# Three resident slices of each half of the second expert weights, and six b in half rows

## The chip, the cores and the metric

The kernel runs on one core of a Trainium2 chip. The metric is the time of one execution on the device in microseconds (us). These units matter here: TensorE does the matrix products (PE, its weight loads PEld), VectorE (DVE), ScalarE (ACT) and GpSimd (POOL) work on elements, SyncE (SP) issues transfers, and 16 DMA engines carry them between HBM and the on-chip memory.

## The reference

Three layers follow each other. An attention over 8 batches b (512 tokens and 32 states each) gives 544 rows of 512 per b. A feed-forward layer with two weights follows, and then a soft mixture of 8 experts. The last one is where the change lies:

```python
logits = x @ phi
d = softmax of logits over the 4608 tokens
slot_input = (d.T @ x).reshape(E, S_per_e, D)
for e in range(E):
    h = np.maximum(slot_input[e] @ w1[e], 0.0)
    slot_out[e] = h @ w2[e]
c = softmax of logits over the 32 slots
return (c @ slot_out).astype(np.float32)
```

w2 is 8 experts of 1024 x 512 in float32, 16.8 MB. Every row of the output, 4608 x 512, is a mix of the 32 rows of slot_out, so nothing can be stored before slot_out is there, at least for a half of the 512 columns.

## The kernel before

The main part, up to about 400 us, runs over the 8 batches (hstep, tstep, estep, smblock); the change doesn't touch it. What follows is a tail.

Weights of the experts come in slices of 1 MB, 128 partitions x 2048. There are 16 of w1 (half an expert's columns each) and 16 of w2: slice e of w2 is the first 256 output columns of expert e, slice 8 + e the last 256. They are loaded by SP into whatever place has come free: give puts places into a list, and prefetch takes the next place for the next slice of the list `slices`. So the order of the list is the order of the loads. The list is the four pieces of the feed-forward weight, the 16 slices of w1, and w2 in `order`:

```python
r0 = CFG["r0"]
kept = [list(range(8 - r0, 8)), list(range(10 + r0, 16))]
order = [i for i in range(16) if i not in kept[0] + kept[1]] + kept[0] + kept[1]
```

The last six of the list are resident: ends loads them early, into six places of the tile gp. With r0 = 0 these are slices 10 to 15.

After w1 (line 1053) two generators do the second product, slot_out(0) for the first 256 columns and slot_out(1) for the last (line 1088), eight steps of one slice each. A last step evicts the sum (tile SO), spreads it with a small product (SR, line 1095) and evicts that into `so`. slot_out takes the resident slices first. The generators combine then do the last product of a group of b: `combine(0, ...)` the first 256 columns of two b at a time, `combine(1, ...)` the last 256, `combine(None, ...)` all 512 columns of one b, for the b in `whole`, and of the rows of the states. They write four PSUM banks (tiles oV, oH, oX, oE), evict them by turns on DVE (line 1128) and ACT, and issue the store on SP (line 1132; the rows of the states on POOL, line 1136). A half-row store is 512 KB in runs of 1 KB, a whole-row store 1 MB in runs of 8 KB.

In which order the generators step is a string of CFG: 0 and 1 are the slot_outs, c is combine(0); afterwards slot_out(1), combine(0), combine(None) and combine(1) are run to their end in this order. The SP queue is worked off in the order of the program, so a store that waits holds up all stores behind it.

Of the kernel before, what the change touches and what calls it, by code (L numbers as in the profile page):

```python
# [13 lines left out]
PSUM = bass.MemoryType.PSUM  # L14


CFG = {'no': 1, 'nl': 0, 'n0': (1, 12), 'nw': 512, 'nj': 'CABD', 'cw': (2, 2, 2, 4, 5, 6, 6, 7, 8, 8, 9, 11, 12, 13, 14, 15), 'pr': (0, 4, 6), 'a0n': 5, 'w1p': (), 'r0': 0, 'sw': 1, 'whole': (4, 5, 6, 7), 'em': 8, 'lE': (0, 5, 8, 11), 'sV': (0, 4, 9, 12), 'sE': (7, 11, 15), 'sS': (1, 3, 5, 7), 'sN': 13, 'sM': (14, 14), 'gv7': 'EESESSSEESSSEEEE', 'cpos': (0, 0, 1, 2, 2, 3, 3, 7, 8, 10, 10, 10, 14, 14), 'at0': (4, 4, 7, 7, 9, 13, 14, 14, 14, 15), 'lP0': ((0, 1), (1, 0), (3, 0), (3, 1)), 'lP1': ((1, 0), (1, 1), (2, 0), (2, 1), (3, 0)), 'gv1': 'EEEEEEEEEESEEEES', 'f32': (0, 1, 2, 3), 'wsm': 14, 'xsP': 1, 'eng': ('PE',), 'wt8': (7, 8, 9, 10, 11, 12, 13, 14), 'wte': 'DA', 'wb': 12, 'gv6': (3, 5, 15), 'lP': ((0, 0), (0, 1), (1, 0), (2, 0), (3, 1)), 'attA': (3, 3, 9, 9, 9, 10, 10, 12), 'attB': (1, 11, 11, 12, 13), 'attN': (14, 15), 'dv': (3, 7, 8), 'fl': -0.484375, 'hp': 2000, 'att7': (3, 5, 6, 7, 8, 10), 'og': 1, 'n3': 1, 'n3m': 10, 'wS': ('DP', 'PP', 'AD', 'PD', 'AP', 'DP', 'AP', 'AD', 'AD', 'DP', 'AD', 'AP', 'AP', 'AD', 'PD', 'AD'), 'xsm': 12, 'k0': 0, 'rg': 6, 'spg': 0, 'att0': 6, 'att': 7, 'V0': (1, 2, 4), 'Vn': (1, 2, 10), 'Vx': 12, 'wn': 'H', 'wsev': 'adad', 'conv': (4, 8, 9, 11, 12, 13, 19, 21, 24, 26, 28, 32, 36, 40, 44, 48, 52, 56, 60), 'todo': [1, 1, 1, 2, 0, 0, 0, 3, 0, 0, 2, 2, 1, 1, 0, 0], 'E0': ((0, 7), (0, 14), (0, 15), (1, 1)), 'T0': ((0, 9), (0, 14), (1, 1), (1, 2)), 'sm0': 6, 'E': 1, 'sm': 1, 'tqB': (5, 9, 13), 'GP': 0, 'pe': (3,), 'psH': 3, 'gtpX': (0, 7), 'tq0': (13, 15), 'keep': (2, 3, 4, 5), 'x2': (1, 0), 'natm': 1, 'warm': 26, 'bounce7': (0, 3), 'split': 1, 'wt': 0, 'so': '1011110001000010c1cc1', 'smm': (0, 0, 1, 2, 8, 10, 12), 'tqv': (), 'tqvm': 0, 'first': 'x', 'apath': 2, 'f32c': 1, 'place': 1, 'attm': (3, 6, 7, 8, 9, 12), 'subPm': True, 'loDm': False, 'bounce': (0, 1, 2, 3), 'bq': ('s', 's'), 'xq': 's', 'nat': ((1, 11), (2, 2), (2, 3), (2, 11), (3, 2), (3, 4), (3, 9), (4, 2), (4, 3), (4, 9), (5, 2), (5, 3), (5, 9), (6, 2), (6, 4), (6, 9)), 'subP': (1,), 'mulD': (), 'loD': (), 'qlag': 0, 'gv0': 'SSEEEEEESEEEEEEE', 'gv': 'EEEEEEESEEEESEEE', 'gvS': 'BEBBBBBBBBBSBEBB'}


@with_exitstack  # L20
def kernel(
# [20 lines left out]
    def pool(name, bufs, **kw):  # L42
        return ctx.enter_context(tc.tile_pool(name=name, bufs=bufs, **kw))
# [6 lines left out]
    small = pool("small", 2)  # L50
    psH = pool("psH", CFG["psH"], space=PSUM)
    psE = pool("psE", 1, space=PSUM)
    psV = pool("psV", 1, space=PSUM)
    psX = pool("psX", 5 - CFG["psH"], space=PSUM)
    dram = pool("dram", 1, space=bass.MemoryType.DRAM)
# [58 lines left out]
    def group(calls, after=(), chain=False):  # L114

        first = mm(**calls[0])  # L116
        for i in after:
            tc.add_manual_dep(first.ins, i.ins.name, SYNC, reason="side by side")
        with tc.high_priority(CFG["hp"]):
            last = first  # L120
# [5 lines left out]
    def act(out, in_, func=ACTF.Copy, **kw):  # L126
        return nc.scalar.activation(out=out, in_=in_, func=func, **kw)  # L127
# [21 lines left out]
    def words(i, dst):  # L149

        w = stage[i].bitcast(U32).rearrange("p (f w) -> p f w", w=2)
        if i in CFG["dv"]:
            d = dst.bitcast(U32)
# [9 lines left out]
        r = rim.bitcast(U8).rearrange("p (f w) -> p f w", w=4)  # L163
        act(r[:, :, 0], b[:, :, 3], scale=2.0 ** -5, bias=CFG["fl"])
        if i in CFG["pr"]:
            nc.gpsimd.tensor_copy(out=r[:, :, 3], in_=b[:, :, 7])
# [1025 lines left out]
```

## Time and profile before

| | us |
|---|---|
| median of 3 runs | 481.89 (480.94 to 482.29) |
| profiled execution | 481.20 |
| its span | 479.4 |
| PE busy | 435.4 |
| DVE busy | 374.4 |
| ACT busy | 289.2 |
| POOL busy | 239.5 |

The span runs from the first to the last record; the profiled execution's own time is 1.8 us longer. Busy times of different engines overlap, and PE, the busiest, has nothing to do in the last 15 us, so shares over the whole span don't tell what sets the end. For that one reads stretches: the share of the DMA engines (a mean of 16, which can read a little above 1), and their rate in GB/s, microsecond by microsecond.

### The profile page before, as it was taken

To read this page: it belongs to the slowest core of one execution; us is meant where nothing else is said; L and a number is where in the kernel's file an instruction comes from. 1 tells how busy PE (TensorE), PEld (TensorE's weight loads), DVE (VectorE), ACT (ScalarE), POOL (GpSimd) and SP (SyncE) were. 2 spreads that over 40 slices of the span, in tenths; PEclk is the share of its full clock that TensorE was granted. 3 is DMA by queue.
4 is the path that set the end of the run, shared out by engine and by line. 5 is a ranking of instruction groups with operands and counts; after the bars stand their busy time and mean duration, and the time that the engine had idled before them with its cause. 6 is when DMAs were issued, how large, how long until landed. Compare 5 with 4: busy or idle time off the path is not lost.

```text
span 479.4 us, 10721 instructions
## 1 busy us (share of the span) xinstructions
PE 435.4 (91%) x4336; PEld 247.3 (52%) x4336; DVE 374.4 (78%) x667; ACT 289.2 (60%) x528; POOL 239.5 (50%) x217
## 2 busy tenths in 40 slices
PE   5689899999999999999999999999999997999850
PEld 2433345456565565655556555565557685435330
DVE  2999999896999998999799899878878655430260
ACT  1876996647775875886697587565654464220350
POOL 4243447865774973885497388464146231220030
PEclk9899999999999999999999999999999999999995
DMA  8999822011403613342351346025053598999698
GB/s 304 420 420 420 338 89 89 19 71 27 151 18 132 250 44 133 114 196 61 127 210 46 133 144 252 3 90 176 2 211 124 198 404 335 349 424 414 255 355 314
DMA packets 19809, 94.21 MB, mean 197 GB/s; under 512 B 1840, under 2 KB 6320, under 8 KB 11184
## 3 DMA queue, kind: packets, MB, share of 16 engines
q1 hardware_dynamic: 19504, 93.00, 51.0%
q8 instruction: 34, 0.56, 0.5%
q0 software_dynamic: 256, 0.52, 0.5%
q14 instruction: 15, 0.12, 0.1%
HBM read 80.41 MB, written 13.11 MB: 195 GB/s over the span
## 4 chain that ended last, share of the span: by engine, by line
PE 49%; DVE 28%; DMA 6%; ACT 5%; issue 5%; POOL 4%; ACTq 0%; SPq 0%; POOLq 0%; DVEq 0%
PE h L538 17%; DVE gp L612 6%; DVE g L592 5%; PE h L546 5%; PE E L116 3%; DMA w<-in_w_dram 3%; PE FV L122 3%; PE V L116 3%; PE h L1053 3%; POOL c L568 2%; PE h L529 2%; PE FX L122 2%; DVE mx L294 2%; DMA wb<-in_won_dram 2%; DVE z L335 1%
## 5 line engine op out<-in xcount | busy, mean ns | idle before, releaser
L538 PE MATMUL h<-a,v 128*128 128x512 f32 x672 | 175.5, 405 | 2.3 <-DVE g L592 2.0
L568 POOL TENSOR_TENSOR c<-c 128x512 f32<-128x512 f32 x106 | 114.6, 1084 | 97.1 <-ACT c L127 95.3
L538 PEld LDWEIGHTS h<-a,v 128*128 128x128 f32 x672 | 120.3, 188 | 77.9 <-issue 19.5
L127 ACT ACTIVATE c<-h,half 128x512 f32<-128x512 f32 x128 | 88.3, 691 | 71.0 <-PE h L538 54.6
L592 DVE SCALAR_TENSOR_TENSOR g<-h,c 128x512 f32<-128x512 f32 x112 | 74.7, 668 | 20.1 <-POOL c L568 17.0
L612 DVE STREAM_TRANSPOSE gp<-g 128x512 f32<-128x512 f32 x112 | 78.0, 699 | 1.1
L485 POOL TENSOR_TENSOR v<-Vs,v 128x512 fp32r<-128x512 f32 x30 | 41.7, 1389 | 9.5 <-ACT Vs L127 9.5
L127 ACT ACTIVATE v<-V 128x512 fp32r<-128x512 f32 (+1 forms) x64 | 38.1, 602 | 8.1 <-PE V L122 4.1
L116 PE MATMUL V<-win,st_t 64*32 64x512 f32 x64 | 34.0, 611 | 4.1 <-ACT att L127 3.7
L122 PE MATMUL V<-win,st_t 64*32 64x512 f32 x448 | 36.3, 612 | 0.0
L122 PE MATMUL FX<-gp,dR 32*32 32x512 f32 x512 | 35.6, 598 | 0.0
L122 PE MATMUL FV<-gp,dR 32*32 32x512 f32 x496 | 35.4, 597 | 0.0
L529 PE MATMUL h<-spare,v 128*128 128x512 f32 x64 | 32.5, 644 | 2.2 <-DVE gp L592 2.0
L122 PE MATMUL E<-g,wp 128*32 128x512 f32 x168 | 29.5, 602 | 0.0
L116 PE MATMUL E<-g,wp 128*32 128x512 f32 x56 | 29.1, 602 | 0.0
L337 POOL TENSOR_TENSOR att<-att,z 128x512 f32<-128x512 f32 x16 | 17.2, 1076 | 18.1 <-DVE z L336 18.1
L546 PE MATMUL h<-XSh,v 128*128 128x256 f32 x128 | 25.2, 289 | 0.1
L127 ACT ACTIVATE spare<-wb 128x512 uint8<-128x512 uint8 x32 | 24.0, 785 | 1.0 <-DMA wb<-in_won_dram 1.0
L1128 DVE COPY o<-oV 128x512 f32<-128x512 f32 x5 | 3.5, 691 | 26.5 <-PE oH L122 26.3
L529 PEld LDWEIGHTS h<-spare,v 128*128 128x128 f32 x64 | 11.9, 202 | 20.2 <-issue 13.5
L546 PEld LDWEIGHTS h<-XSh,v 128*128 128x128 f32 x128 | 20.2, 189 | 2.6 <-DVE g L592 0.8
L375 POOL TENSOR_TENSOR a<-att,a 128x512 fp32r<-128x512 f32 x14 | 19.6, 1418 | 1.1 <-ACT a L127 1.1
(245 smaller groups left out, 813.9 us busy)
## 6 DMA issues: line engine op xcount, KB each, us to landing
w<-in_w_dram SPq DMA_DIRECT2D x22, 1024.0 KB, 9.6
xn<-in_xn_dram SPq DMA_DIRECT2D x8, 1024.0 KB, 4.8
wb<-in_won_dram SPq DMA_DIRECT2D x8, 1024.0 KB, 5.0
xs<-in_xs_dram SPq DMA_DIRECT2D x7, 1024.0 KB, 4.8
gp<-in_w_dram SPq DMA_DIRECT2D x6, 1024.0 KB, 7.4
gp<-in_wout_dram SPq DMA_DIRECT2D x5, 1024.0 KB, 11.7
wb<-in_win_dram SPq DMA_DIRECT2D x4, 1024.0 KB, 12.8
wo<-wb SPq DMA_DIRECT2D x8, 512.0 KB, 3.7
```

The source lines that it names most:

```text
L116: first = mm(**calls[0])
L122: e = mm(**c)
L127: return nc.scalar.activation(out=out, in_=in_, func=func, **kw)
L337: (nc.vector if b in CFG["mulD"] else nc.gpsimd).tensor_tensor(out=t3, in0=t3, in1=z1.unsqueeze(2).to_broadcast([128, 16, 32]), op=ALU.mult)
L375: (nc.vector if b in CFG["loD"] or b > 1 and CFG["loDm"] else nc.gpsimd).tensor_tensor(out=lo[:, G, :], in0=raw[G], in1=hi[:, G, :], op=AL ...
L485: nc.gpsimd.tensor_tensor(out=lo[:, G, :], in0=Vs, in1=hi[:, G, :], op=ALU.subtract)
L529: mm(out=h, lhsT=Vt[0, c][0][:, G, 128 * mm_:128 * mm_ + 128], rhs=araw[0][G], start=(G == 0), stop=(G == 1))
L538: mm(out=h, lhsT=v[:, G, f], rhs=a[:, G, :], start=(k == 0), stop=(k == 5))
L546: mm(out=h, lhsT=w[:, j, :], rhs=x[:, j, :], start=(k == 0), stop=(k == 11))
L568: nc.gpsimd.tensor_tensor(out=c, in0=c, in1=c, op=ALU.mult)
L592: gI[b, m] = nc.vector.scalar_tensor_tensor(out=g, in0=h, scalar=1.0, in1=c, op0=ALU.max, op1=ALU.min)
L612: nc.vector.transpose(out=gd_of(b, m), in_=gT[b, m])
```

## The change

Three entries of CFG are changed; no other line is.

```diff
 CFG = {
...
-'r0': 0, 'sw': 1, 'whole': (4, 5, 6, 7),
+'r0': 3, 'sw': 1, 'whole': (6, 7),
...
-'so': '1011110001000010c1cc1',
+'so': '111000000000ccc111111',
...
```

With r0 = 3 the resident slices are 5, 6, 7 and 13, 14, 15, and the ten others are loaded in the order 0 to 4, 8 to 12. With whole = (6, 7) the b 0 to 5 are combined in pairs and stored in half rows, and 6 and 7 in whole ones. The string runs the three resident steps of slot_out(1), all of slot_out(0), the three pairs of combine(0), and the rest of slot_out(1).

On PE, at the end of slot_out(0): w_5_4620 is slice 5 of w2 (the last number is that of the buffer), SO the sum, SR its spreading, oV the first bank of the combine. Lines with - are before, with + after.

```order
-L1088 MATMUL SO<-w_5_4620,hTD 32x256 x8
-L1088 MATMUL SO<-w_6_4626,hTD 32x256 x8
-L1088 MATMUL SO<-w_7_4632,hTD 32x256 x8
-L1088 MATMUL SO<-w_8_4638,hTD 32x256 x4
+L1088 MATMUL SO<-w_8_4620,hTD 32x256 x8
 L1095 MATMUL SR<-tail,cst_t 128x256
-L1088 MATMUL SO<-w_8_4639,hTD 32x256 x4
+L1088 MATMUL SO<-w_9_4626,hTD 32x256 x8
 L116 MATMUL oV<-tail,LT 128x256
 L122 MATMUL oV<-tail,LT 128x256
```

The first half's SR stood behind slice 7 and half of slice 8, the eighth and ninth of the ten that are loaded; it now stands behind slices 4 and 8, the fifth and sixth, and the first combine behind slice 9, the seventh.

On PE, right behind the first pairs of the combine:

```order
-L1088 MATMUL SO<-w_9_4646,hTD 32x256 x8
+L1088 MATMUL SO<-w_10_4632,hTD 32x256 x8
 L122 MATMUL oH<-tail,LT 128x256 x2
+L116 MATMUL oV<-tail,LT 128x256
+L122 MATMUL oV<-tail,LT 128x256
+L122 MATMUL oH<-tail,LT 128x256
+L122 MATMUL oV<-tail,LT 128x256 x2
+L122 MATMUL oH<-tail,LT 128x256
+L1088 MATMUL SO<-w_11_4638,hTD 32x256 x4
+L1088 MATMUL SO<-w_11_4639,hTD 32x256 x2
+L122 MATMUL oH<-tail,LT 128x256 x2
+L1088 MATMUL SO<-w_11_4639,hTD 32x256 x2
```

The last piece of the second pair stands behind the eighth loaded slice (10; before it was 9, the tenth), and the third pair is put between it and the two halves of slice 11.

On SP, the end of the queue, from the last six loads on:

```order
-L1132 DMA out_dram<-o 512x1x256 x4
-L1132 DMA out_dram<-o 128x2048 x4
-L1132 DMA out_dram<-o 512x1x256 x4
+L814 DMA w_8_4620<-in_w_dram 128x2048
+L814 DMA w_9_4626<-in_w_dram 128x2048
+L814 DMA w_10_4632<-in_w_dram 128x2048
+L814 DMA w_11_4638<-in_w_dram 128x1024
+L814 DMA w_11_4639<-in_w_dram 128x1024
+L814 DMA w_12_4646<-in_w_dram 128x2048
+L1132 DMA out_dram<-o 512x1x256 x6
+L1132 DMA out_dram<-o 128x2048 x2
+L1132 DMA out_dram<-o 512x1x256 x6
```

The loads keep their sizes, buffers and order under other names (slices 5 to 9 before, 8 to 12 now), and behind them stand six, two and six stores instead of four, four and four.

## Rows read from the trace of the kernel before

**Rows 1.** The page's part 2: DMA busy tenths in 40 slices.
```profile
DMA  8999822011403613342351346025053598999698
```

**Rows 2.** Windows: length, busy of five engines, PE clock, DMA share, GB/s.
```profile
431.00:447.00 16.00, 13.17 (x232) 7.13 (x232) 0.00 (x0) 0.77 (x2) 0.00 (x0) 1.00 1.02 417
...
453.00:477.00 24.00, 8.72 (x69) 4.75 (x68) 8.14 (x13) 7.25 (x15) 4.08 (x8) 0.80 1.02 362
```

**Rows 3.** Windows of one microsecond, between loads and stores.
```profile
448.00:449.00 1.00, 1.00 (x20) 0.59 (x16) 0.00 (x0) 0.23 (x1) 0.00 (x0) 1.00 0.40 164
449.00:450.00 1.00, 1.00 (x21) 0.92 (x16) 0.43 (x1) 0.00 (x0) 0.00 (x0) 1.00 0.12 49
450.00:451.00 1.00, 1.00 (x20) 0.42 (x16) 1.00 (x3) 0.71 (x2) 0.00 (x0) 1.00 0.00 0
451.00:452.00 1.00, 1.00 (x11) 0.62 (x4) 1.00 (x2) 1.00 (x3) 0.00 (x0) 1.00 0.00 0
452.00:453.00 1.00, 1.00 (x5) 0.34 (x3) 0.05 (x1) 0.66 (x2) 0.00 (x0) 1.00 0.29 99
```

**Rows 4.** Timeline of PE (start us, us), slot_out; in brackets idle time and releaser.
```profile
431.45 1.07 PE L1088 MATMUL SO<-gp,hTD 128*32 128x256 f32 x16 [0.52 <-ACT hTD L127]
...
440.11 1.91 PE L1088 MATMUL SO<-w,hTD 128*32 128x256 f32 x32
442.77 1.07 PE L1088 MATMUL SO<-w,hTD 128*32 128x256 f32 x16 [0.75 <-DMA w<-in_w_dram]
445.28 1.07 PE L1088 MATMUL SO<-w,hTD 128*32 128x256 f32 x16 [1.44 <-DMA w<-in_w_dram]
...
447.81 0.64 PE L1088 MATMUL SO<-w,hTD 128*32 128x256 f32 x8
...
450.32 1.07 PE L1088 MATMUL SO<-w,hTD 128*32 128x256 f32 x16
```

**Rows 5.** Timeline of PE and SP: the first combine and its store.
```profile
448.38 0.48 PE L116 MATMUL oV<-tail,LT 32*128 32x256 f32 x1
...
451.40 0.64 SPq L1132 DMA_DIRECT2D out_dram<-o  x1
```

**Rows 6.** Windows of a quarter microsecond: the loads' end and the stores' end.
```profile
447.75:448.00 0.25, 0.25 (x5) 0.16 (x8) 0.00 (x0) 0.15 (x1) 0.00 (x0) 1.00 1.10 459
448.00:448.25 0.25, 0.25 (x8) 0.00 (x0) 0.00 (x0) 0.23 (x1) 0.00 (x0) 1.00 0.47 197
...
449.25:449.50 0.25, 0.25 (x11) 0.23 (x6) 0.00 (x0) 0.00 (x0) 0.00 (x0) 1.00 0.23 98
449.50:449.75 0.25, 0.25 (x10) 0.23 (x6) 0.18 (x1) 0.00 (x0) 0.00 (x0) 1.00 0.00 0
...
477.50:477.75 0.25, 0.00 (x0) 0.00 (x0) 0.00 (x0) 0.00 (x0) 0.00 (x0) 0.50 0.23 78
```

**Rows 7.** Windows of stores: half rows, then states among others, whole rows, half rows.
```profile
453.00:456.00 3.00, 2.06 (x13) 0.70 (x12) 1.28 (x3) 1.01 (x4) 0.00 (x0) 1.00 1.03 339
...
461.00:463.00 2.00, 2.00 (x22) 1.46 (x20) 1.93 (x5) 1.12 (x3) 0.00 (x1) 1.00 0.99 268
...
464.00:468.00 4.00, 0.00 (x0) 0.00 (x0) 0.00 (x0) 0.68 (x2) 0.00 (x0) 0.90 1.00 363
468.00:472.00 4.00, 0.00 (x0) 0.00 (x0) 0.00 (x0) 0.00 (x0) 0.00 (x0) 0.50 0.99 400
...
469.00:471.00 2.00, 0.00 (x0) 0.00 (x0) 0.00 (x0) 0.00 (x0) 0.00 (x0) 0.50 1.02 430
...
472.00:477.00 5.00, 0.00 (x0) 0.00 (x0) 0.00 (x0) 0.00 (x0) 0.00 (x0) 0.50 1.05 353
```

**Rows 8.** Timeline of PE and SP: the second half, to the first whole-row store.
```profile
451.32 1.13 PE L122 MATMUL oH<-tail,LT 32*128 32x256 f32 x4
...
453.55 0.69 PE L116 MATMUL oV<-tail,LT 32*128 32x512 f32 x1 [0.47 <-ACT tail L127]
...
456.56 0.35 SPq L1132 DMA_DIRECT2D out_dram<-o  x1
```

More of the change, by code (lines that the diff above doesn't have):

```diff
@@ L14 @@
 PSUM = bass.MemoryType.PSUM
-CFG = {'no': 1, 'nl': 0, 'n0': (1, 12), 'nw': 512, 'nj': 'CABD', 'cw': (2, 2, 2, 4, 5, 6, 6, 7, 8, 8, 9, 11, 12, 13, 14, 15), 'pr': (0, 4, 6), 'a0n': 5, 'w1p': (), 'r0': 0, 'sw': 1, 'whole': (4, 5, 6, 7), 'em': 8, 'lE': (0, 5, 8, 11), 'sV': (0, 4, 9, 12), 'sE': (7, 11, 15), 'sS': (1, 3, 5, 7), 'sN': 13, 'sM': (14, 14), 'gv7': 'EESESSSEESSSEEEE', 'cpos': (0, 0, 1, 2, 2, 3, 3, 7, 8, 10, 10, 10, 14, 14), 'at0': (4, 4, 7, 7, 9, 13, 14, 14, 14, 15), 'lP0': ((0, 1), (1, 0), (3, 0), (3, 1)), 'lP1': ((1, 0), (1, 1), (2, 0), (2, 1), (3, 0)), 'gv1': 'EEEEEEEEEESEEEES', 'f32': (0, 1, 2, 3), 'wsm': 14, 'xsP': 1, 'eng': ('PE',), 'wt8': (7, 8, 9, 10, 11, 12, 13, 14), 'wte': 'DA', 'wb': 12, 'gv6': (3, 5, 15), 'lP': ((0, 0), (0, 1), (1, 0), (2, 0), (3, 1)), 'attA': (3, 3, 9, 9, 9, 10, 10, 12), 'attB': (1, 11, 11, 12, 13), 'attN': (14, 15), 'dv': (3, 7, 8), 'fl': -0.484375, 'hp': 2000, 'att7': (3, 5, 6, 7, 8, 10), 'og': 1, 'n3': 1, 'n3m': 10, 'wS': ('DP', 'PP', 'AD', 'PD', 'AP', 'DP', 'AP', 'AD', 'AD', 'DP', 'AD', 'AP', 'AP', 'AD', 'PD', 'AD'), 'xsm': 12, 'k0': 0, 'rg': 6, 'spg': 0, 'att0': 6, 'att': 7, 'V0': (1, 2, 4), 'Vn': (1, 2, 10), 'Vx': 12, 'wn': 'H', 'wsev': 'adad', 'conv': (4, 8, 9, 11, 12, 13, 19, 21, 24, 26, 28, 32, 36, 40, 44, 48, 52, 56, 60), 'todo': [1, 1, 1, 2, 0, 0, 0, 3, 0, 0, 2, 2, 1, 1, 0, 0], 'E0': ((0, 7), (0, 14), (0, 15), (1, 1)), 'T0': ((0, 9), (0, 14), (1, 1), (1, 2)), 'sm0': 6, 'E': 1, 'sm': 1, 'tqB': (5, 9, 13), 'GP': 0, 'pe': (3,), 'psH': 3, 'gtpX': (0, 7), 'tq0': (13, 15), 'keep': (2, 3, 4, 5), 'x2': (1, 0), 'natm': 1, 'warm': 26, 'bounce7': (0, 3), 'split': 1, 'wt': 0, 'so': '1011110001000010c1cc1', 'smm': (0, 0, 1, 2, 8, 10, 12), 'tqv': (), 'tqvm': 0, 'first': 'x', 'apath': 2, 'f32c': 1, 'place': 1, 'attm': (3, 6, 7, 8, 9, 12), 'subPm': True, 'loDm': False, 'bounce': (0, 1, 2, 3), 'bq': ('s', 's'), 'xq': 's', 'nat': ((1, 11), (2, 2), (2, 3), (2, 11), (3, 2), (3, 4), (3, 9), (4, 2), (4, 3), (4, 9), (5, 2), (5, 3), (5, 9), (6, 2), (6, 4), (6, 9)), 'subP': (1,), 'mulD': (), 'loD': (), 'qlag': 0, 'gv0': 'SSEEEEEESEEEEEEE', 'gv': 'EEEEEEESEEEESEEE', 'gvS': 'BEBBBBBBBBBSBEBB'}
@@ new lines @@
+CFG = {'no': 1, 'nl': 0, 'n0': (1, 12), 'nw': 512, 'nj': 'CABD', 'cw': (2, 2, 2, 4, 5, 6, 6, 7, 8, 8, 9, 11, 12, 13, 14, 15), 'pr': (0, 4, 6), 'a0n': 5, 'w1p': (), 'r0': 3, 'sw': 1, 'whole': (6, 7), 'em': 8, 'lE': (0, 5, 8, 11), 'sV': (0, 4, 9, 12), 'sE': (7, 11, 15), 'sS': (1, 3, 5, 7), 'sN': 13, 'sM': (14, 14), 'gv7': 'EESESSSEESSSEEEE', 'cpos': (0, 0, 1, 2, 2, 3, 3, 7, 8, 10, 10, 10, 14, 14), 'at0': (4, 4, 7, 7, 9, 13, 14, 14, 14, 15), 'lP0': ((0, 1), (1, 0), (3, 0), (3, 1)), 'lP1': ((1, 0), (1, 1), (2, 0), (2, 1), (3, 0)), 'gv1': 'EEEEEEEEEESEEEES', 'f32': (0, 1, 2, 3), 'wsm': 14, 'xsP': 1, 'eng': ('PE',), 'wt8': (7, 8, 9, 10, 11, 12, 13, 14), 'wte': 'DA', 'wb': 12, 'gv6': (3, 5, 15), 'lP': ((0, 0), (0, 1), (1, 0), (2, 0), (3, 1)), 'attA': (3, 3, 9, 9, 9, 10, 10, 12), 'attB': (1, 11, 11, 12, 13), 'attN': (14, 15), 'dv': (3, 7, 8), 'fl': -0.484375, 'hp': 2000, 'att7': (3, 5, 6, 7, 8, 10), 'og': 1, 'n3': 1, 'n3m': 10, 'wS': ('DP', 'PP', 'AD', 'PD', 'AP', 'DP', 'AP', 'AD', 'AD', 'DP', 'AD', 'AP', 'AP', 'AD', 'PD', 'AD'), 'xsm': 12, 'k0': 0, 'rg': 6, 'spg': 0, 'att0': 6, 'att': 7, 'V0': (1, 2, 4), 'Vn': (1, 2, 10), 'Vx': 12, 'wn': 'H', 'wsev': 'adad', 'conv': (4, 8, 9, 11, 12, 13, 19, 21, 24, 26, 28, 32, 36, 40, 44, 48, 52, 56, 60), 'todo': [1, 1, 1, 2, 0, 0, 0, 3, 0, 0, 2, 2, 1, 1, 0, 0], 'E0': ((0, 7), (0, 14), (0, 15), (1, 1)), 'T0': ((0, 9), (0, 14), (1, 1), (1, 2)), 'sm0': 6, 'E': 1, 'sm': 1, 'tqB': (5, 9, 13), 'GP': 0, 'pe': (3,), 'psH': 3, 'gtpX': (0, 7), 'tq0': (13, 15), 'keep': (2, 3, 4, 5), 'x2': (1, 0), 'natm': 1, 'warm': 26, 'bounce7': (0, 3), 'split': 1, 'wt': 0, 'so': '111000000000ccc111111', 'smm': (0, 0, 1, 2, 8, 10, 12), 'tqv': (), 'tqvm': 0, 'first': 'x', 'apath': 2, 'f32c': 1, 'place': 1, 'attm': (3, 6, 7, 8, 9, 12), 'subPm': True, 'loDm': False, 'bounce': (0, 1, 2, 3), 'bq': ('s', 's'), 'xq': 's', 'nat': ((1, 11), (2, 2), (2, 3), (2, 11), (3, 2), (3, 4), (3, 9), (4, 2), (4, 3), (4, 9), (5, 2), (5, 3), (5, 9), (6, 2), (6, 4), (6, 9)), 'subP': (1,), 'mulD': (), 'loD': (), 'qlag': 0, 'gv0': 'SSEEEEEESEEEEEEE', 'gv': 'EEEEEEESEEEESEEE', 'gvS': 'BEBBBBBBBBBSBEBB'}
```

## The prediction

> **What bounds the kernel now.** I read the page first, then the windows of stretches, then the end of the timeline. In 40 slices the DMA line is at 8 and 9 from slice 32 on with one exception, a 6 in slice 37 [rows 1]. PE, DVE and ACT are nearly empty in the last slices. So the end of this kernel is set by the 16 DMA engines: they load the last slices of w1 and w2 and then store 8.9 MB of output. Two windows show it: from 431 to 447 us they are fully busy with loads at 417 GB/s, from 453 to 477 us fully busy with stores at 362 GB/s [rows 2]. What bounds the end is then a sum, bytes by rate, plus every stretch in which the engines have nothing to do. There is one. From 448 to 453 us the shares of the five microseconds are 0.40, 0.12, 0, 0 and 0.29 [rows 3], so 5 - 0.81 = 4.2 us of a mean engine are lost. That is the 6 of slice 37.
>
> The reader is to see why it is there. Every store of output needs slot_out of at least one half of w2 (line 1088), and before the change the first half needs slices 0 to 7, which are the last but two to be loaded. PE runs through the slices that are there in one go from 431.45 to 442.02 us (12 slices, 0.88 us each), then it waits for each next one: it starts at 442.77, 445.28, 447.81 and 450.32 us, each time released by the load [rows 4]. The first half is complete at 445.28 + 1.07 = 446.35, its combine starts at 448.38, and the first store is issued at 451.40 [rows 5]. The loads have drained by then and nothing else is queued.
>
> **What the change does, part by part.**
>
> *Which slices are resident.* The six places in gp hold 5, 6, 7 of each half instead of six of the second. Number, size, order and place of the loads stay; only their names change. Up to 431 us nothing moves: 0. The SP loads are the same rows in the same order, with slices 8, 9, 10, 11, 12 in the positions of 5, 6, 7, 8, 9, so they land at the times of the trace.
>
> *First half earlier.* It now needs six resident slices' worth of PE work (three of each half, queued first) and 0 to 4: 11 slices by 0.88 = 9.7 us, from 431.45 to 441.1. The loads don't hold it, since PE takes slices 4 and 5 without a wait until 442.02 [rows 4], and slice 4 is reached at the same point as before. From the end of slot_out to its combine the trace has 448.38 - 446.35 = 2.03 us, which gives 443.2; but slice 9 now stands ahead of the combine on PE and arrives when slice 6 did, at 442.77, so the combine starts at 443.65. From its start to the first store the trace has 451.40 - 448.38 = 3.02 us [rows 5]: first store at 446.7 instead of 451.4. Issue to first bytes took 451.40 to about 452.75 (share 0.29 in the last microsecond, [rows 3]), 1.35 us; that gives 448.0, when the first engines run out of loads [rows 6]. Of the groups for b 2, 3 and 4, 5 pieces stand on PE behind slices 10 and 11, which arrive at 445.28 and 447.81, and their stores follow by an estimated 1.5 us each (two evictions of 0.7 on DVE beside two on ACT); each pair is 1.05 MB, 3.0 us of store, so DMA doesn't catch up with them.
>
> *How much of the gap is won.* The loads do not end together: the share falls from 1.10 to 0.47 at 448.0, is 0.23 until 449.5, and 0 after it [rows 6]. Most engines idle 452.75 - 448.2 = 4.5 us, the last ones 452.75 - 449.5 = 3.25. The stores end closer together: 0.23 in the quarter before 477.75 is the last of them [rows 6]. With no pause between, the late engines stay late, and the last engine sets the end. Bounds: 3.25 and 4.5. I take 3.6, nearer to the late engines.
>
> *Half rows for b 4 and 5.* 2.1 MB change from 8 KB to 1 KB runs. Windows with half rows alone ran at 339 and 353 GB/s, whole rows alone at 430, windows in which whole rows meet others at 363 and 400 [rows 7]. 2.1 MB take 2.1/0.346 = 6.1 us in half rows and 2.1/0.430 = 4.9 (pure) to 2.1/0.38 = 5.5 (mixed) in whole ones: 0.6 to 1.2 us more. I take 1.0, nearer to the pure window. The lower end of the range is 0, for the case below.
> The Trainium skill (DMA: Bandwidth & Descriptors, Specifications) says that runs from 512 B up move at line rate. By it this term is 0. The trace doesn't agree: 353 against 430 GB/s at 1 KB and 8 KB, so the sum goes by the rows.
>
> *More stores on SP.* Twelve half-row stores and two whole ones instead of eight and four. A half-row issue takes SP 0.64 us, a whole-row one 0.35 [rows 5, 8]; the bytes of a half-row store take 524288/0.346 = 1.52 us, so SP stays ahead: 0. Queued behind the six on SP is the whole-row store of b 6. It needs the second half: slice 12 starts at 450.32 like slice 9 before, where the combine of the first whole row followed at 453.55 and its store at 456.56 [rows 8]. So 456.6 at most; 0.7 less if the piece of combine that PE did in between (from 451.32 on [rows 8]) is out of the way, 455.9. Its first bytes come at 457.2 to 457.9. The six stores are 3.15 MB, 9.1 us, and last from 448.1 (late engines 449.5) to 457.2 (458.6). So this fits with nothing to spare, and what is late next, if anything, is b 6.
>
> *Evictions after that.* Five groups and the state are left instead of six and the state. Before, DVE was through at 464 and ACT had 0.68 us left [rows 7], with 13 us of stores still to go; they end earlier now. 0.
>
> Sum: -3.6 + 1.0 = -2.6 us. The profiled execution took 481.20 us (span 479.4 and 1.8 around it), which becomes 478.6; it is 0.7 under the median of the runs, 481.89, and I put the difference on that: **479.3**. Own range of the forecast: -4.5 + 0.6 = -3.9 to -3.25 + 1.2 = -2.05, so 478.0 to 479.8.
>
> **The rivals.** *Half rows are free*: a 1 KB run costs the engines what the same bytes of an 8 KB run cost, and the 339 to 353 GB/s belong to those moments and not to the row length. For it: a window that was mostly whole rows fell to 363 too. Against: two stretches 20 us apart agree. -3.6 + 0 gives 478.3. The rule of the Trainium skill quoted above (DMA: Bandwidth & Descriptors, Specifications) would have it so.
>
> *The gap moves.* The first stores share the engines with slices 11 and 12, slice 12 lands late, and b 6, which has nothing to spare, leaves a hole between 457 and 459. If one half-row store goes ahead of the slice on each engine, 1.52 us: -2.6 + 1.5 gives 480.8; a hole of up to 1.1 still leaves it faster by 0.3%. For it: the tight sum above. Against: all stores stand behind all loads on SP's one queue, and the loads of the last 1 MB each landed at an even pace, 2.5 us apart [rows 4].
>
> *The first half doesn't start earlier.* The change doesn't do what it says if the combine of the first half still waits for the late slices, since its pieces stand on PE behind slices 9, 10 and 11. Then only the price is left: +1.0, 482.9. Against: only the last pieces stand behind 10 and 11, and these land by 447.8.
>
> *Slower: half rows fall further when more of them are queued.* Between 461 and 463 us, where the state rows from POOL's queue meet the others, the rate was 268 GB/s [rows 7]. The first half has six stores of 1 KB runs in line instead of four and the second six. If all 6.3 MB of half rows ran at 268 and not at 346, they would take 23.5 and not 18.2 us, +5.3 - 2.6 = +2.7: 484.6. It decides from 6.3/(18.2 + 2.6 + 1.45) = 283 GB/s down, where the time is 0.3% above the median. For it: that one row. Against: the last five microseconds, half rows alone and four stores deep, held 353 [rows 7].
>
> **How the numbers follow.** A measurement of this kernel tells about 0.3%, 1.45 us, from no change. Forecast 0.62, half rows free 0.12, moved gap 0.14, no earlier start 0.07, slower half rows 0.05. Faster by over 0.3% (under 480.44): 0.62 + 0.12 + half of 0.14 = 0.81. Within 0.3%: the other half and 0.07, 0.14. Slower: 0.05. The range holds the first three: from 477.6 (the 3.9 of the bound and 0.4 of spread, as the runs lie) to 480.8.
>
> **What would show it.** In the profile of the changed kernel: the windows from 448 to 452 us have DMA shares near 1; the first store is issued near 446.7 and the first half's slot_out ends near 441.1; PE starts slice 12 near 450.3; the store of b 6 is issued at 456 to 456.6 and no window from 456 to 460 falls below 0.9; half-row windows stay at 340 to 355 GB/s; the stores end near 475. Wrong if the window from 448 to 452 stays empty, if a hole opens near 457, or if half rows run under 300.

## The result and the profile after

The changed kernel takes 477.9 us (median of 6 executions, 477.2 to 479.1); the kernel before, executed beside it, 482.09 (median of 6). The ratio is 0.9918, with a 95% interval from 0.9896 to 0.994. So it is faster by 4.2 us, where 2.6 were forecast; 477.9 lies in the range, near its lower end. The profiled execution of the changed kernel took 477.84 us (span 476.1), 3.4 less than the 481.20 of before.

The page's part 2 and part 6 of the changed kernel (busy tenths of the DMA engines and their rate in 40 slices; then issues, KB each, median us to landing):

```profile
DMA  8999822010404613251361336115043598999998
GB/s 306 420 421 419 350 89 89 19 72 21 159 9 137 250 49 134 96 215 32 116 253 47 134 105 251 45 58 210 2 178 132 187 383 298 377 419 419 365 354 295
...
out_dram<-o SPq DMA_DIRECT2D x12, 512.0 KB, 5.8
```

The 6 in slice 37 of [rows 1], counted from 0, has become a 9: from slice 32 on the DMA engines have work until the end. Twelve half-row stores are issued where there were eight.

Windows of one microsecond of the changed kernel, from the loads' end past the store of b 6, and at the stores' end (length, busy of PE, PEld, DVE, ACT, POOL, PE clock, DMA share, GB/s):

```profile
446.00:447.00 1.00, 1.00 (x18) 0.42 (x17) 1.00 (x3) 0.69 (x2) 0.00 (x0) 1.00 1.10 455
447.00:448.00 1.00, 1.00 (x20) 0.66 (x16) 1.00 (x2) 0.89 (x2) 0.00 (x0) 1.00 0.65 270
448.00:449.00 1.00, 1.00 (x22) 0.48 (x16) 0.46 (x2) 0.50 (x1) 0.00 (x0) 1.00 0.44 165
449.00:450.00 1.00, 1.00 (x10) 0.56 (x5) 0.90 (x2) 0.70 (x2) 0.00 (x0) 1.00 1.04 346
...
455.00:456.00 1.00, 0.68 (x4) 0.00 (x0) 1.00 (x2) 0.40 (x1) 0.00 (x0) 1.00 1.10 361
456.00:457.00 1.00, 0.75 (x8) 0.50 (x10) 0.76 (x2) 1.00 (x3) 0.00 (x0) 1.00 0.95 324
457.00:458.00 1.00, 1.00 (x16) 0.74 (x10) 0.58 (x1) 0.17 (x1) 0.94 (x2) 1.00 1.17 406
...
471.00:474.00 3.00, 0.00 (x0) 0.00 (x0) 0.00 (x0) 0.00 (x0) 0.00 (x0) 0.50 1.03 346
474.00:475.00 1.00, 0.00 (x0) 0.00 (x0) 0.00 (x0) 0.00 (x0) 0.00 (x0) 0.50 0.29 99
```

Read the last two columns. The pause of [rows 3], five microseconds with shares of 0.40, 0.12, 0, 0 and 0.29, is now two microseconds with 0.65 and 0.44: 0.91 us of a mean engine in place of 4.2. Behind it the engines are full, also where b 6 has to follow the six half-row stores (455 to 458). The stores, at 346 GB/s, end between 474 and 475, against 477.75 in [rows 6].

The timeline of PE and of SP in the changed kernel (start us, us; in brackets idle time and releaser), which answers to [rows 4], [rows 5] and [rows 8]:

```profile
430.59 7.07 PE L1088 MATMUL SO<-gp,hTD 128*32 128x256 f32 x96 [0.52 <-ACT hTD L127]
437.48 5.36 PE L1088 MATMUL SO<-w,hTD 128*32 128x256 f32 x96
442.78 0.70 PE L1095 MATMUL SR<-tail,cst_t 128*128 128x256 f32 x2
443.41 1.07 PE L1088 MATMUL SO<-w,hTD 128*32 128x256 f32 x16
444.41 0.48 PE L116 MATMUL oV<-tail,LT 32*128 32x256 f32 x1
...
450.55 1.49 PE L1088 MATMUL SO<-w,hTD 128*32 128x256 f32 x20
...
447.42 0.63 SPq L1132 DMA_DIRECT2D out_dram<-o  x1
...
456.71 0.35 SPq L1132 DMA_DIRECT2D out_dram<-o  x1
```

The first half's spreading (L1095) runs at 442.78 and the first store is issued at 447.42, 4.0 us earlier than the 451.40 of before. The first line of the timeline tells why it isn't more: the six resident slices took 6.9 us (430.59 to 437.48), where six slices at the 0.88 us of the prediction are 5.3. Windows of 8 us over this place, of the changed kernel in this execution and in another (e1_again, below):

```profile
430.00:438.00 8.00, 7.48 (x109) 4.13 (x112) 0.00 (x0) 0.38 (x1) 0.00 (x0) 0.79 1.02 419
```

```profile
430.00:438.00 8.00, 7.48 (x138) 4.46 (x141) 0.00 (x0) 0.38 (x1) 0.00 (x0) 1.00 1.02 417
```

The granted clock (third number from the end) was 0.79 in the mean here, so TensorE was at the lower of its two levels for part of the stretch, and 1.00 there. This is not part of the change. It is told at e1_again what it cost.

### The profile page after: what moved, and what is told of

Its sections match the earlier page's. It is cut to its first block, busy times and chain, and to the rows that moved or that the text cites. A ratio compares the mean times of both kernels' runs of the same rounds, so it can differ in the third digit from the quotient of the medians.

```text
span 476.1 us, 10757 instructions
## 1 busy us (share of the span) xinstructions
PE 439.7 (92%) x4352; PEld 250.3 (53%) x4352; DVE 374.4 (79%) x667; ACT 290.2 (61%) x528; POOL 240.5 (51%) x217
## 4 chain that ended last, share of the span: by engine, by line
PE 59%; DVE 27%; issue 4%; ACT 4%; POOL 3%; DMA 1%; ACTq 0%; SPq 0%; POOLq 0%; DVEq 0%
PE h L538 19%; DVE gp L612 6%; DVE g L592 5%; PE h L546 5%; PE E L116 4%; PE FV L122 4%; PE SO L1088 4%; PE V L116 3%; PE h L1053 3%; PE h L529 3%; PE FX L122 2%; DVE mx L294 2%; PE FV L116 1%; DVE win L172 1%; DVE z L335 1%
## 5 line engine op out<-in xcount | busy, mean ns | idle before, releaser
L116 PE MATMUL V<-win,st_t 64*32 64x512 f32 x64 | 33.4, 601 | 3.6 <-ACT att L127 3.4
L529 PE MATMUL h<-spare,v 128*128 128x512 f32 x64 | 34.1, 668 | 1.8 <-DVE spare L360 1.1
L122 PE MATMUL V<-win,st_t 64*32 64x512 f32 x448 | 35.7, 601 | 0.0
L1136 POOL DMA_DIRECT2D out_dram<-o x8 | 4.1, 518 | 32.6 <-DVE o L1128 32.6
```

The source lines that it names most:

```text
L122: e = mm(**c)
L529: mm(out=h, lhsT=Vt[0, c][0][:, G, 128 * mm_:128 * mm_ + 128], rhs=araw[0][G], start=(G == 0), stop=(G == 1))
```

## The experiments

The question was first whether the gain has the two terms of the sum (pause won, half-row price), then where the rest of the 4.2 us comes from. One measure serves throughout: the **tail**, from slot_out's first product on PE to the end of the span. All terms of the sum lie in it. What moves ahead of slot_out shifts both of its ends, and touches it only as far as the loads don't shift along. For the kernel before it is 479.4 - 431.45 = 47.9 us, for the changed kernel 476.1 - 430.59 = 45.5. Two explanations for what the sum doesn't hold were carried along: that the other residency shortens the part ahead of slot_out (C), and that executions of before with a lower TensorE clock are longer (E).

**The changed kernel again (e1_again).** No edit; a second trace, and more timed executions.

> The changed kernel once more, unchanged. In its first profile TensorE's granted clock was 0.79 from 430 to 438 us where the kernel before had 1.00, slot_out's resident part took 6.9 us in place of 5.3, and the first store was issued at 447.4, 1.6 us later than worked out. Theory A (that drop is an accident of one execution): without it the first store comes 16.0 us or less after slot_out's first product (451.40 - 431.45 = 19.95 before, 16.83 in the first profile, 15.25 worked out), the pause of DMA between loads and stores is under 0.3 us in place of 0.9, and the time lies near 478 us. Theory B (the drop belongs to the new order on PE): clock again about 0.8 from 430 to 438, first store again 16.8 us after slot_out's start. Rival C (part of the gain lies upstream of slot_out): slot_out starts again near 430.6 and not 431.5.

477.54 us against 481.24 for the kernel before, ratio 0.9908 [0.989, 0.9927] (the quotient of the two medians is 0.9923). Timeline of PE and SP, and windows:

```profile
430.65 5.39 PE L1088 MATMUL SO<-gp,hTD 128*32 128x256 f32 x96 [0.52 <-ACT hTD L127]
...
442.49 1.07 PE L1088 MATMUL SO<-w,hTD 128*32 128x256 f32 x16 [0.64 <-DMA w<-in_w_dram]
...
446.50 1.31 SPq L1132 DMA_DIRECT2D out_dram<-o  x2
...
447.00:448.00 1.00, 1.00 (x21) 0.53 (x15) 0.46 (x2) 0.41 (x1) 0.00 (x0) 1.00 0.86 351
448.00:449.00 1.00, 1.00 (x12) 0.51 (x5) 0.98 (x2) 0.76 (x2) 0.00 (x0) 1.00 1.02 370
...
473.50:473.75 0.25, 0.00 (x0) 0.00 (x0) 0.00 (x0) 0.00 (x0) 0.00 (x0) 0.50 0.31 107
...
474.50:474.75 0.25, 0.00 (x0) 0.00 (x0) 0.00 (x0) 0.00 (x0) 0.00 (x0) 0.50 0.07 25
474.75:475.00 0.25, 0.00 (x0) 0.00 (x0) 0.00 (x0) 0.00 (x0) 0.00 (x0) 0.50 0.06 20
```

With the clock at 1.00 slot_out's resident part takes 5.2 us (430.65 to 435.85), slice 9 now waits for its load (0.64 us), as the prediction had it, and the first store is issued 15.85 us after slot_out's start instead of 16.83. The pause is closed: 0.86, then 1.02. Yet the tail is 476.4 - 430.65 = 45.7, no shorter than with a pause of 0.9 us. The last rows show why: the mean engine is done near 473.6, but a share of 0.07, about a sixteenth and so the work of about one engine, goes on to 475. In the first trace the engines ended nearly together:

```profile
474.00:474.25 0.25, 0.00 (x0) 0.00 (x0) 0.00 (x0) 0.00 (x0) 0.00 (x0) 0.50 0.76 258
474.25:474.50 0.25, 0.00 (x0) 0.00 (x0) 0.00 (x0) 0.00 (x0) 0.00 (x0) 0.50 0.37 127
474.50:474.75 0.25, 0.00 (x0) 0.00 (x0) 0.00 (x0) 0.00 (x0) 0.00 (x0) 0.50 0.04 12
```

So closing the last 0.9 us of the mean engine's pause gained nothing at the end here; the last engine sets it. A further trace (e7_again, no edit) has both again.

> The changed kernel, unchanged, a third trace. Theory A: tail 45.5 to 45.8 us; slot_out may start later than 431. Rival C: slot_out starts between 430.4 and 431.0 once more. Clock from 430 to 438: 1.00 if the drop of the first profile was an accident.

477.88 us, tail 476.1 - 430.99 = 45.1, clock 1.00 from 430 to 438, first store after 15.43 us. Windows:

```profile
447.00:448.00 1.00, 1.00 (x22) 0.48 (x16) 0.46 (x2) 0.50 (x1) 0.00 (x0) 1.00 0.90 366
...
474.25:474.50 0.25, 0.00 (x0) 0.00 (x0) 0.00 (x0) 0.00 (x0) 0.00 (x0) 0.50 0.07 25
474.50:474.75 0.25, 0.00 (x0) 0.00 (x0) 0.00 (x0) 0.00 (x0) 0.00 (x0) 0.50 0.05 16
```

The pause is 0.1 us, and a share of 0.07 again trails, to 474.75. Counted from slot_out's start, the mean engine is done after 43.7 us in the first trace and after 42.9 and 42.4 in the two with the pause closed (worked out from the quarter windows); the last engine ends within 44.2, 44.4 and 43.8. The mean engine gained 0.8 and 1.3 us, the end nothing and 0.4. The changed kernel's three tails are 45.5, 45.7 and 45.1, mean 45.4.

**Half rows alone (e2_half_only).** The kernel before, with b 4 and 5 in half rows and nothing else (of CFG only the entry is shown, here and below):

```diff
-'whole': (4, 5, 6, 7),
+'whole': (6, 7),
```

> The kernel before with b 4 and 5 in half rows, and nothing else: residents 10 to 15 as before. Theory A (a price of half rows by rate, 349 against 430 GB/s): first store at 451.4 as before, stores last 0.8 to 1.2 us longer, so 0.8 to 1.2 us slower than before, ratio 1.002. Rival (half rows are free): 0, ratio 1.000. Rival (half rows also help, since the whole rows need the second half and the first stores bridge a wait): a gain, ratio under 1.000.

482.31 us, ratio 1.002 [1.0004, 1.0037]: 1.07 us longer than before in the same comparison. Its tail is 481.4 - 432.29 = 49.1, against a mean of 48.4 for before (below): 0.7. Windows, one among the first stores and one of half rows alone:

```profile
455.00:456.00 1.00, 0.22 (x5) 0.16 (x8) 0.00 (x0) 0.79 (x3) 0.00 (x0) 1.00 0.74 246
...
472.00:477.00 5.00, 0.00 (x0) 0.00 (x0) 0.00 (x0) 0.00 (x0) 0.00 (x0) 0.50 1.05 349
```

349 GB/s with six stores in line, as 353 in [rows 7] with four. So half rows have a price, and it doesn't grow with the number queued. One microsecond, at 455, has a share of 0.74 and takes 0.26 us of the 0.7 in this trace, so the rows themselves cost 0.4 to 1.07. The rival of slower half rows falls clearly. Free ones don't fit either, but by little: the interval begins at 1.0004, and the tail is a single one, of an execution (483.22 us) above the median.

**Early first half alone (e3_early_only).** The changed kernel with four whole rows, so only two pairs of half rows lie between the loads and b 4:

```diff
-'r0': 3, 'sw': 1, 'whole': (6, 7),
+'r0': 3, 'sw': 1, 'whole': (4, 5, 6, 7),
...
-'so': '111000000000ccc111111',
+'so': '111000000000cc111111',
```

> The changed kernel with b 4 to 7 in whole rows as before: residents 5, 6, 7 of each half, only two pairs in half rows. Theory A: the first store comes as early as in the changed kernel (447.4), but four stores of 0.5 MB last only 6.1 us, to about 454, and the first whole-row store can't be issued before 456.7: a new pause of 3 us or more near 455. So most of the gain is lost: between 0 and 1.0 us faster than before, ratio 0.998 to 1.000, 3 us slower than the changed kernel. Rival (the half rows of b 4 and 5 only cost): 1.0 us faster than the changed kernel, ratio 0.990.

479.76 us, ratio 0.9968 [0.995, 0.9987]. Windows:

```profile
453.00:454.00 1.00, 1.00 (x10) 0.39 (x4) 0.20 (x1) 0.00 (x0) 0.00 (x0) 1.00 0.68 236
454.00:455.00 1.00, 0.61 (x4) 0.00 (x0) 1.00 (x2) 0.48 (x1) 0.00 (x0) 1.00 0.24 79
455.00:456.00 1.00, 0.83 (x8) 0.51 (x11) 0.68 (x2) 1.00 (x3) 0.00 (x1) 1.00 0.00 0
456.00:457.00 1.00, 1.00 (x12) 0.30 (x5) 0.66 (x2) 0.09 (x1) 1.00 (x2) 1.00 0.63 262
```

The first pause is gone and a new one is there: 0.32 + 0.76 + 1 + 0.37 = 2.45 us, before the first whole row. Four half-row stores don't reach to it. This is the hole of the rival "the gap moves", and the two half-row stores more in the changed kernel are what fills it. The time is 1.5 us shorter than before (481.24 in this comparison), where 0 to 1.0 were expected, and 2.2 longer than the 477.54 of the changed kernel, where 3 were: the hole was expected at 3 us or more. The 12 timed executions lie in two groups, 478.4 to 478.9 and 480.7 to 481.8, six each, which led to the three further traces below.

**Five instead of six (e6_w3).** The changed kernel with `'whole': (5, 6, 7)`; the string is unchanged.

> The changed kernel with three b in whole rows (5, 6, 7) and five in half rows: one first-half store of 0.5 MB fewer in the bridge. Theory A (the bridge of six stores has nothing to spare): five stores last 7.6 us from 447.6, to about 455.2, the whole-row store of b 5 is issued 25.1 us after slot_out's start as that of b 6 was, near 455.8, with first bytes near 457: a pause of 1.3 to 1.8 us, less 0.5 for 1 MB that goes in whole rows, so 0.8 to 1.3 us slower than the changed kernel. Rival (the bridge has slack): 0.5 us faster than the changed kernel, no pause.

479.4 us, ratio 0.9951 [0.9933, 0.997]. Windows:

```profile
456.00:457.00 1.00, 1.00 (x12) 0.54 (x15) 0.47 (x1) 0.89 (x2) 0.21 (x1) 1.00 0.39 122
457.00:458.00 1.00, 1.00 (x12) 0.23 (x5) 0.86 (x2) 0.08 (x1) 1.00 (x3) 1.00 0.91 377
```

A hole of 0.61 + 0.09 = 0.7 us where the changed kernel has 0.95 and 1.17. So the bridge needs its sixth store: the changed kernel has less than one store to spare. The hole is smaller than the 1.3 to 1.8 us expected. The tail is 476.6 - 430.63 = 46.0, only 0.5 longer than the first trace's; this trace had the lowered clock at 430 to 438 (0.79), too. It is the shortest execution of the eight, 478.37 us; by medians the kernel is 1.5 us longer than the changed one (477.9), above the 0.8 to 1.3 expected.

**One slice more (e5_r4).** The changed kernel with four resident slices of the first half and two of the second:

```diff
-'r0': 3,
+'r0': 4,
...
-'so': '111000000000ccc111111',
+'so': '110000000000ccc1111111',
```

> The changed kernel with residents 4 to 7 of the first half and 14, 15 of the second, so that the first half needs four loaded slices and the second six. Theory A: the first half is complete one slice's work (0.9 us) earlier or at least free of a late clock drop, the pause of 0.9 us between loads and stores goes, nothing else moves: 0.5 to 1.0 us faster than the changed kernel, ratio to before 0.990. Rival (the pause isn't set by the first half's completion, but by issue and the engines' ends): the same as the changed kernel within 0.3 us. Rival (the second half becomes late): PE reaches slice 13 as late as it reached slice 12, so this should not show; if it does, a pause near 457.

477.59 us, ratio 0.9911 [0.9892, 0.993], tail 476.8 - 430.97 = 45.8: the changed kernel's time, and not the 0.5 to 1.0 us less that were expected. Timeline of PE:

```profile
442.96 1.07 PE L1088 MATMUL SO<-w,hTD 128*32 128x256 f32 x16 [0.78 <-DMA w<-in_w_dram]
```

The slice more didn't bring the first store forward: it is issued at 446.97, 16.0 us after slot_out's start, as against 15.85 in e1_again. On PE the combine still stands behind a slice for whose load PE waits 0.78 us. So this run doesn't tell what an earlier first store would be worth.

**The kernel before again (b1_again, b2_again, b3_again).** No edit; its tail, to see whether 47.9 is typical.

> The kernel before, unchanged, to have a second trace of its tail and the spread of equal kernels. From slot_out's first product to the end of the span its profile had 47.95 us; the changed kernel had 45.48 and 45.75 in two profiles, so the tail shows 2.2 to 2.5 us, while the timed runs show 3.6 to 4.2. Theory A (the rest is spread of the part ahead of slot_out, which the change doesn't touch): tail again 47.9 us within 0.3, slot_out starts anywhere from 430.4 to 432.3, ratio 1.000 within 0.002. Rival C (the changed kernel is shorter ahead of slot_out): slot_out starts at 431.4 to 432.3 in every profile of this kernel and at 430.4 to 431.0 in every one of the changed one. Rival D (the first profile of this kernel had a short tail): tail of 49 us.

> The kernel before, unchanged, a third trace. Theory A: tail 47.9 us within 0.3. Rival C: slot_out starts at 431.4 or later. Rival D: tail of 49 us.

> The kernel before, unchanged, a fourth trace. Its 56 timed runs correlate with the mean granted TensorE clock of the run (0.978 and more: 481.2 us on average; less: 482.6), those of the changed kernel do not. Theory E (a clock drop behind slot_out's start stands in the path of this kernel's tail, where PE waits for loads and then feeds the stores): if the clock of this run is under 0.975, a window between 440 and 462 us shows a clock under 1.00 and the tail is over 49 us; if not, the tail is 47.9 to 48.7 as in the three traces so far. Rival: a low clock with the drop in the first 60 us only, and a tail of 48.3.

482.22 (ratio 0.9997 [0.9974, 1.0021]), 482.18 and 481.73 us; the tails are 480.3 - 431.66 = 48.6, 480.3 - 431.98 = 48.3 and 480.0 - 431.22 = 48.8. With the first, the mean is 48.4. The execution on which the prediction rests had the shortest tail of the four. The first store is issued 19.95 us after slot_out's start in the first trace and 20.37, 20.05 and 20.35 in these, so the short tail goes with an early first store. No trace of before had a lowered clock in the tail while PE had work, so E is neither shown nor refuted by them. But b2_again, with a mean clock of 0.973, had its low stretches in the first 60 us (0.91 there, 1.00 from 60 to 464) and a tail of 48.3: a low mean clock alone doesn't point to the tail.

**Three more traces of e3 (e3_t1, e3_t2, e3_t3).** No edit against e3_early_only.

> The changed kernel with b 4 to 7 in whole rows, as in e3_early_only, for its trace. Its 12 timed runs lie in two groups, 478.4 to 478.9 and 480.7 to 481.8 us; its first profile, 478.67, is of the lower one, with slot_out starting at 430.4 and a tail of 46.4 us. Theory A (the spread arises ahead of slot_out, in the part that the change doesn't touch): if this run falls in the upper group, slot_out starts 2 us later, near 432.5, and the tail is 46.4 within 0.4. Rival D (the spread arises in the tail): slot_out starts near 430.5 and the tail is 48 us or more.

> The same kernel, one more trace. Theory A: the tail is 46.4 us within 0.4 in either group, and slot_out's start carries the difference. Rival D: the tail carries it.

> The same kernel, one more trace. Theory A: the tail is 46.4 us within 0.4 in either group, and slot_out's start carries the difference. Rival D: the tail carries it.

479.62, 480.62 and 479.69 us. slot_out starts at 431.40, 430.51 and 431.75 (430.43 in e3_early_only). That overlaps before's spread (431.22 to 431.98) with the changed kernel's residency, but over all traces a lean remains: five with the old residency (e2_half_only among them) begin at 431.2 to 432.3, nine with a new one at 430.4 to 431.8. What settles C is how old this lean is. The first loads of w2, two resident slices, are the first transfers that differ. The timeline of SP, before and changed:

```profile
348.12 0.80 SPq L814 DMA_DIRECT2D gp<-in_w_dram  x2
```

```profile
347.29 0.80 SPq L814 DMA_DIRECT2D gp<-in_w_dram  x2
```

They are issued at 348.32, 348.68 and 347.91 in the other traces of before, at 347.34 and 347.67 in those of the changed kernel, and in each of the fourteen traces slot_out starts 83.2 to 83.4 us later. So the whole difference is there before anything that the change alters has run, and C falls: the residency doesn't shorten the part ahead.

Of the tails, 46.4, 48.3 and 46.0, the second stands out. Windows, slot_out's last slice and the store of the first whole row in e3_t1, then the same in e3_t2, with the first combine of that row:

```profile
450.00:455.00 5.00, 3.38 (x30) 1.41 (x30) 0.44 (x1) 0.77 (x2) 0.00 (x0) 1.00 0.97 332
455.00:460.00 5.00, 3.98 (x32) 1.95 (x32) 4.27 (x8) 3.64 (x7) 3.24 (x7) 1.00 0.59 226
...
450.64 1.07 PE L1088 MATMUL SO<-w,hTD 128*32 128x256 f32 x16 [1.43 <-DMA w<-in_w_dram]
...
456.40 0.35 SPq L1132 DMA_DIRECT2D out_dram<-o  x1
```

```profile
448.00:449.00 1.00, 0.00 (x0) 0.00 (x0) 0.00 (x0) 0.00 (x0) 0.00 (x0) 1.00 1.04 380
...
450.00:455.00 5.00, 4.04 (x24) 1.56 (x16) 0.00 (x0) 0.77 (x2) 0.00 (x0) 0.50 0.76 264
455.00:460.00 5.00, 5.00 (x24) 1.51 (x18) 2.88 (x5) 1.78 (x4) 1.70 (x4) 0.51 0.38 156
...
449.49 1.81 PE L1088 MATMUL SO<-w,hTD 128*32 128x256 f32 x16 [1.51 <-DMA w<-in_w_dram]
453.48 1.22 PE L116 MATMUL oV<-tail,LT 32*128 32x512 f32 x1 [0.47 <-ACT tail L127]
...
457.44 0.35 SPq L1132 DMA_DIRECT2D out_dram<-o  x1
```

In e3_t2 PE had nothing to do from 448 to 449, while slice 12 was awaited. From 450 to 460 the granted clock was 0.50, that is 1.2 GHz instead of 2.4. The last slice began 1.15 us earlier than in e3_t1 and took 1.81 us instead of 1.07, the combine's products 1.22 where [rows 8] have 0.69, and the store was issued 1.0 us later than in e3_t1. The engines, out of half rows, waited: shares of 0.76 and 0.38 against 0.97 and 0.59. The tail is 2 us longer. So in this trace a lowered clock in the tail cost time, because the stores waited for PE. The two groups of e3_early_only fit it: its six long executions have mean clocks of 0.969 to 0.975, five of the six short ones 0.976 or more.

## Why the prediction came out as it did

**The bound: right.** The end is bytes by rate plus the time in which the DMA engines have nothing to do. Loads and stores moved at the rates of before (419 and 346 GB/s, against 417 and 353), and PE's longer busy time (439.7 us, 435.4 before) doesn't show in the tail: 45.5 with the lowered clock, 45.7 and 45.1 without. The output has 8 x 544 = 4352 rows of 512, which are the 8.9 MB of the prediction; the 4608 given for the tokens and the output's rows is not this kernel's number.

**First half earlier: right, a little late.** Forecast was the first store at 446.7, which is 15.25 us after slot_out's start. Without the lowered clock it was 15.85 and 15.43; in the first trace 16.83. The slices, the wait for slice 9 and the path to the store were as worked out; what the step left out is that the clock can fall in these 5 us. It cost 1.7 us on PE, of which 0.7 was taken back where slice 9 no longer had to be waited for. One reading of the step is wrong: of the four starts of PE that it says the loads released, 447.81 and 450.32 show no such wait; there PE came from the spreading and from the first pieces of the combine. The first store hangs on 442.77, which was released by a load, and slice 12, in the row that begins at 450.55, came near the forecast all the same.

**How much of the gap is won: right, as far as the tails tell.** The step said that the late engines count and took 3.6 us. By the means of the tails the change gives 45.4 - 48.4 = -3.0 us, and the tails of the two kernels don't overlap (45.1 to 45.7, 47.9 to 48.8). With the price of half rows at 0.4 to 1.1, the part won is 3.4 to 4.1: within the bounds of the step, and the 3.6 with it. That the last engine counts, and not the mean one, is borne out by e1_again and e7_again: they close a pause that the first trace still had, and the end comes 0.4 us sooner at most.

**Half rows: right in size.** Forecast +1.0, measured 0.4 to 1.07 (e2_half_only), at 346 to 349 GB/s. An estimate from e3 gives 1.1: its three traces at full clock have 2.3 us of hole on average (2.45, 2.3 and 2.3) where the changed kernel's have 0.4 (0.9, 0.1 and 0.1), but a tail only 0.8 to 0.9 longer (46.3 against 45.4), and what is missing the changed kernel pays for its two b more in half rows. So the rule of the Trainium skill that runs from 512 B on move at line rate (DMA: Bandwidth & Descriptors, Specifications) doesn't describe these stores: the measurement decides, and 1 KB runs are slower than the 430 GB/s of 8 KB runs in [rows 7].

**b 6's store fits with nothing to spare: right.** It was issued at 456.71 for a forecast of 456 to 456.6, with the lowered clock; at the full clock at 455.79 and 455.71, which is 25.1 and 24.7 us after slot_out's start for a forecast of 24.5 to 25.1. No window from 456 to 460 is under 0.95 in the first trace. e6_w3 shows the margin: one store less leaves 0.7 us empty, e3_early_only two less 2.45. The rival "the gap moves" had the right place, but needs a shorter bridge than the changed kernel has. "The first half doesn't start earlier" fell with the first store.

**Where the 4.2 us come from: the sum came out 1.6 us short.** It was made against one execution, 481.20 us, and put the part ahead at nothing: "up to 431 us nothing moves: 0". Three things stand against the 1.6.
- The tail. That execution's tail of 47.9 is the shortest of four (mean 48.4), so the changed tail was set against a value 0.5 too low. In the tails the change gives -3.0 where -2.6 was forecast. This is the part that the mechanism accounts for.
- The part ahead. slot_out starts 0.8 us earlier in the mean of the changed kernel's three traces (430.7) than in the four of before (431.6). The sentence holds as far as it speaks of the change, since the whole 0.8 is older than the first load that differs; as a forecast of the time, 0 was wrong by it. Why these traces lean that way stays open. The two together are 3.8 us.
- The rest, between 3.8 and the 4.2 and 3.7 of the two comparisons by medians, lies within their intervals and needs no cause.

So 477.9 lies in the range by the mechanism and by 0.8 us that aren't the mechanism's: without them it would be nearer to the forecast.

The clock (E) remains as a candidate for the spread of the executions. Each timed execution has a mean granted clock. Of 58 executions of before in these comparisons, the 33 at 0.978 or more took 481.2 us in the mean, the 25 below 482.6; of 13 of the changed kernel, the 10 at 0.978 or more took 477.9, the 3 below 477.6. At the high clock the difference is 3.3 us. The changed kernel may be less sensitive since stores lie ready while PE is slow, and the first trace's lowered clock indeed left its tail at 45.5; e3_t2 lost 2 us where none lay ready. But that is e3's chain and not that of before, and for before there is only the correlation, which b2_again doesn't bear out. It isn't shown.

No variant beat the changed kernel; e5_r4 equals it.

## What to carry to other kernels

Where the DMA engines set the end, look for the microseconds in which they have no work, and ask which slice the first store waits for: choosing other resident slices moves it without moving a byte. Then count the stores that must bridge to the next ones, since a bridge that is one store short opens the pause again further on. Before a sum is made against one profiled execution, take a second: here the tail of the same kernel differed by 0.8 us between traces, a third of the forecast. And before a difference is put down to a change, look where in the program it first shows: a shift that is older than the first instruction that differs isn't the change's doing.

## What the runs showed of the hardware

- TensorE's granted clock fell in the midst of work, in the first trace of the changed kernel and in e6_w3 at 430 to 438 us, where the other traces of the changed kernel had 1.00 after the same work. In e3_t2 it fell behind a wait of PE of 1.51 us; e3_t1 had a wait for the same load (1.43 us) and kept 1.00. What decides it these rows don't tell. At the lower level the six resident slices took 6.9 us in place of 5.2, with the mean clock of the 8 us at 0.79.
- The DMA engines don't always end together: a share of 0.07, about one engine of 16, went on for a microsecond after the rest in e1_again (to 475) and e7_again (to 474.75). So a mean share near 1 doesn't say when the last byte lands.
